# A gated feed-forward kernel: a load of x that waits for a memset, and fillers of another size

## The chip, the cores and the metric

The kernel runs on one core of a Trainium2 chip. The core has five engines with a queue each: TensorE (PE; its weight loads are listed apart as PEld), VectorE (DVE), ScalarE (ACT), GpSimd (POOL) and SyncE (SP). Transfers between the chip's memory and the core's on-chip memory are issued by an engine's queue (here SP and ACT) and carried out by 16 DMA engines. The metric is the device time of one execution in microseconds (us): 163.03 us before, the median of 3 runs that went from 162.87 to 163.18.

## The reference

```python
def reference(x, w_gate, w_up, w_down):
    g = _silu(x @ w_gate)
    u = x @ w_up
    return (g * u) @ w_down
```

All arrays are bf16: x is 1 x 2048 x 640 (S = 2048 rows, D = 640), w_gate and w_up are 640 x 1536 (F = 1536), w_down is 1536 x 640.

## The kernel before

**Tiles.** The 2048 rows are worked in four blocks of 512 (`sb`). D is cut into five parts of 128 (`kd`), F into twelve of 128 (`fc`, `kf`). For each block and each fc, line 197 (`proj`) adds up five matmuls of 512 columns for the gate (`pg`) and five for the up projection (`pu`); line 214 takes the silu on ScalarE, line 215 multiplies on VectorE into `aT`. After twelve fc the block is multiplied with `w_down` (lines 273 and 302), copied and stored. Beside this VectorE works out the last four rows of x by dot products (line 150).

TensorE needs x turned, with D on the partitions (`xT`). Rows 0 to 255 are loaded as they lie, into `x_sb` (line 85: rows 0 to 127 from SyncE's queue, rows 128 to 255 from ScalarE's), and turned by TensorE against an identity (line 188, five transposes for each 128 rows); ScalarE and VectorE copy the result to `xT` (line 193). The rest of x is turned by the transfer itself (line 109, `turn_x`).

**The order at the start**, which the change touches:

- SyncE's queue: x rows 0 to 127 (line 85); w_gate kd = 0 and, after it, kd = 1 and kd = 4, each for the first four fc (line 120); the turned x rows 256 to 511 (line 109); then w_up (line 82), the rest of w_gate and w_up, and w_down (line 128).
- ScalarE's queue: x rows 128 to 255 (line 85); w_gate kd = 2 and 3 in one transfer (line 120); then a silu on one column of `ones` (line 122), which makes ScalarE load its table early; then its share of the copies (line 193).
- VectorE: the memset of `ones` (line 105), then its copies (line 193).
- TensorE, an order written out by hand in `head` and fixed by `keep_order`: the fillers (`warm`, line 179), matmuls of `ones` with itself whose result nobody reads; ten transposes; the kd = 0 matmuls of the first four fc, first for rows 0 to 127 and then for rows 128 to 255 (line 240, 128 columns); kd = 1 to 4 for rows 0 to 255 (line 240, 256 columns); the same four fc for rows 256 to 511 (line 197, 256 columns); then w_up for these fc (line 197).

The fillers wait for the memset, the transposes for x, line 240 for w_gate and the copies. The function `_trim` takes away the barrier at the beginning, so each engine starts its queue by itself.

Of the kernel before, what the change touches and what calls it, by code (L numbers as in the profile page):

```python
# [10 lines left out]
def _body(  # L11
# [8 lines left out]
    nc = tc.nc  # L20
    P = nc.NUM_PARTITIONS
    f32 = mybir.dt.float32
    bf16 = mybir.dt.bfloat16
    ACT = mybir.ActivationFunctionType
# [10 lines left out]
    S_BLK = 512  # L35
# [1 line left out]
    SUB = S_BLK // P  # L37
    DA = 512
    Q = 32
    N_WARM, N_EARLY = 18, 4  # L40
    T = 4
    WT_STEP = 4
    PE_X = 2
# [4 lines left out]
    consts = ctx.enter_context(tc.tile_pool(name="consts", bufs=1))  # L48
# [7 lines left out]
    x_sb = consts.tile([P, PE_X, D], bf16)  # L56
# [15 lines left out]
    x_v = x2.rearrange("(c p) d -> p c d", p=P)  # L72
# [5 lines left out]
    def wslice(a, b):  # L78
        return slice(a * P, b * P)

    def load_w(eng, dst, src, a, b):
        eng.dma_start(out=dst[:, :, wslice(a, b)], in_=src[:, :, wslice(a, b)])

    def load_x(eng, c0, c1):
        eng.dma_start(out=x_sb[:, c0:c1, :], in_=x_v[:, c0:c1, :])  # L85

    def issue_order(a, b):
        tc.add_manual_dep(
# [8 lines left out]
    def keep_order(engine):  # L97

        traced = [i for i in nc.cur_bb.bb.instructions if i.engine == engine]
        for a, b in zip(traced, traced[1:]):  # L100
            issue_order(a, b)

    ones = consts.tile([P, P], bf16)
    silu_first = consts.tile([P, 1], f32)
    nc.vector.memset(ones[:], 1.0)  # L105

    def turn_x(c0, c1):
        s_sl = slice(c0 * P, c1 * P)
        nc.sync.dma_start_transpose(out=xT[:, :, s_sl], in_=xt_v[s_sl])

    f_sl = wslice(0, N_EARLY)
    load_x(nc.sync, 0, 1)
    load_x(nc.scalar, 1, 2)
    for eng, k0, k1 in (
        (nc.sync, 0, 1),
        (nc.scalar, 2, 4),
# [2 lines left out]
    ):  # L119
        eng.dma_start(out=wg_sb[:, k0:k1, f_sl], in_=wg_v[:, k0:k1, f_sl])  # L120
    turn_x(PE_X, SUB)
    nc.scalar.activation(silu_first[:], ones[:, 0:1], ACT.Silu)
    load_w(nc.sync, wu_sb, wu_v, 0, N_EARLY // 2)
    load_w(nc.sync, wu_sb, wu_v, N_EARLY // 2, N_EARLY)
    for a, b in W_CHUNKS:
# [6 lines left out]
    def turn_w(dst, src):  # L132
# [7 lines left out]
        out=x_row[:],  # L140
        in_=x2[S - T : S, :].rearrange("t d -> (t d)").partition_broadcast(P),
# [32 lines left out]

    pw = psum.tile([P, S_BLK], f32, tag="gu", name="pw", bufs=4)

    def warm(n):
        for _ in range(n):
            nc.tensor.matmul(  # L179
                pw[:, 0:P], lhsT=ones[:], rhs=ones[:], start=True, stop=True  # L180
            )

    def transpose_chunk(c, parts):
        c_sl = slice(c * P, (c + 1) * P)
        for copy, tag, k0, k1 in parts:
            pt = psum.tile([P, k1 - k0, P], bf16, tag=tag, name="pt")
            for kd in range(k0, k1):
                nc.tensor.transpose(  # L188
                    out=pt[:, kd - k0, :],
                    in_=x_sb[:, c, kd * P : (kd + 1) * P],  # L190
                    identity=ident[:],
                )
            copy(out=xT[:, k0:k1, c_sl], in_=pt[:])  # L193

    def proj(ps, w_sb, fc, sb, c0, c1):
        for kd in range(KD):
            nc.tensor.matmul(  # L197
                ps[:, c0:c1],
                lhsT=w_sb[:, kd, fc * P : (fc + 1) * P],
                rhs=xT[:, kd, sb * S_BLK + c0 : sb * S_BLK + c1],  # L200
                start=(kd == 0),
                stop=(kd == KD - 1),
            )
# [6 lines left out]
    def gate(pg, pu, sb, fc, n_s):  # L210

        s0 = sb * S_BLK
        sg = work.tile([P, S_BLK], f32, name="sg")
        nc.scalar.activation(sg[:, 0:n_s], pg[:, 0:n_s], ACT.Silu)  # L214
        nc.vector.tensor_tensor(  # L215
            out=aT[:, fc, s0 : s0 + n_s], in0=sg[:, 0:n_s], in1=pu[:, 0:n_s], op=ALU.mult
        )

    def head():

        dve, act = nc.vector.tensor_copy, nc.scalar.copy
        split = [(act, "po_a", 0, 2), (dve, "po_b", 2, KD)]
        late = PE_X * P
        warm(N_WARM)
        transpose_chunk(0, split)
        transpose_chunk(1, split)  # L230
        pg = [
            psum.tile([P, S_BLK], f32, tag="gu", name="pg", bufs=4)
            for _ in range(N_EARLY)
        ]
        early = [(0, 0, P), (0, P, late)] + [(kd, 0, late) for kd in range(1, KD)]
        for kd, c0, c1 in early:
            for fc in range(N_EARLY):


                nc.tensor.matmul(  # L240
                    pg[fc][:, c0:c1],
                    lhsT=wg_sb[:, kd, wslice(fc, fc + 1)],
                    rhs=xT[:, kd, c0:c1],
                    start=(kd == 0 and c0 == 0),
                    stop=(kd == KD - 1),
                )
        for fc in range(N_EARLY):
            proj(pg[fc], wg_sb, fc, 0, late, S_BLK)
        for fc in range(N_EARLY):
            pu = psum.tile([P, S_BLK], f32, tag="po_b" if fc % 2 else "po_a", name="pu")  # L250
            proj(pu, wu_sb, fc, 0, 0, S_BLK)
            gate(pg[fc], pu, 0, fc, S_BLK)
        keep_order(mybir.EngineType.PE)
        keep_order(mybir.EngineType.Activation)

    head()
    for sb in range(NSB):
        n_s = S_BLK if sb < NSB - 1 else S_BLK - T
# [13 lines left out]
        for kf in range(KF):  # L272
            nc.tensor.matmul(  # L273
                po_t[:],
                lhsT=wd_sb[:, kf, DA:D],
                rhs=aT[:, kf, sb * S_BLK : sb * S_BLK + n_t],
                start=(kf == 0),
                stop=(kf == KF - 1),
# [6 lines left out]
        for q in range(P // Q):  # L285
            nc.scalar.dma_start(
                out=out2[
                    sb * S_BLK : sb * S_BLK + n_t, DA + q * Q : DA + (q + 1) * Q
                ].rearrange("(i r) c -> r i c", r=Q),
                in_=ot_q[q * Q : (q + 1) * Q, :].rearrange("r (i c) -> r i c", c=Q),  # L290
            )

        for j in range(SUB):
            s0 = sb * S_BLK + j * P
            last = sb == NSB - 1 and j == SUB - 1
            cols = [(0, DA, "po_a")]
            if last:
                cols = [(0, DA // 2, "po_a"), (DA // 2, DA, "po_a"), (DA, D, "po_b")]
            for c0, c1, tag in cols:
                po = psum.tile([P, c1 - c0], f32, tag=tag, name="po_a")  # L300
                for kf in range(KF):
                    nc.tensor.matmul(  # L302
                        po[:],
                        lhsT=aT[:, kf, s0 : s0 + P],
                        rhs=wd_sb[:, kf, c0:c1],
                        start=(kf == 0),
                        stop=(kf == KF - 1),
                    )
                ot = outp.tile([P, c1 - c0], bf16, name="ot" if c1 < D else "ot_b")
                if c1 < D:  # L310
                    nc.scalar.copy(ot[:], po[:])  # L311
                    eng = nc.sync
                else:
                    nc.vector.tensor_copy(out=ot[:], in_=po[:])  # L314
                    eng = nc.scalar
# [81 lines left out]
def kernel(tc, *args):  # L397
    _body(tc, *args)
    tc.close()
    tc.compile()  # L400
    _trim(tc.nc)
# [30 lines left out]
```

## Time and profile before

| what | us |
|---|---|
| median of 3 runs | 163.03 |
| profiled execution, device time | 163.16 |
| profiled execution, span from first to last instruction | 161.8 |
| TensorE busy (share of the span) | 158.9 (98%) |
| VectorE busy | 110.9 (69%) |
| ScalarE busy | 42.7 (26%) |
| 18 fillers on TensorE (line 179), from 0.40 | 2.10 |
| memset of `ones` on VectorE (line 105) | 0.165 |

The span begins with SyncE's first issue, at 0.00. The profile is one execution, taken by the hardware profiler. Times in its views are us from the start of the span; "idle before, releaser" says how long an engine stood still and what ended that. Matmuls are pipelined, so the length of one is more than the distance from one start to the next. The chain of waits is followed back from the last instruction: at each step to what released it, or to the instruction before it on its engine.

### The profile page before, as it was taken

How to read it: one execution, taken by the hardware profiler on the slowest of the kernel's cores; microseconds unless marked ns; L12 is line 12 of the kernel's file. 1: busy time of each engine (PE TensorE's matmuls, PEld its weight loads, DVE VectorE, ACT ScalarE, POOL GpSimd, SP SyncE). 2: the span in 40 equal slices, each digit the busy share in tenths (PEclk: the TensorE clock that was granted, in tenths of full speed). 3: DMA queues.
4: the chain of work that ended last, by engine and by line, in shares of the span. 5: the costliest groups of instructions: out<-in, count | busy, mean ns of one | idle time of the engine just before them, and what ended most of it. 6: DMA issues, size and time to landing. Idle time of an engine off the chain costs nothing.

```text
span 161.8 us, 2113 instructions
## 1 busy us (share of the span) xinstructions
PE 158.9 (98%) x796; PEld 77.1 (48%) x796; DVE 110.9 (69%) x249; ACT 42.7 (26%) x74; POOL 0.6 (0%) x6
## 2 busy tenths in 40 slices
PE   8999999999999999999999999999999999999995
PEld 7754444444444444444444444444444444445454
DVE  1035223599469999989919999979964999993000
ACT  5131222112222222211222322221214222222121
POOL 1000000000000000000000000000000000000000
DMA  7999999995189991003110000000321000000312
GB/s 226 265 344 350 363 218 231 245 189 101 35 186 166 228 226 39 4 0 34 65 65 0 0 4 2 0 0 4 61 67 34 0 0 0 0 0 4 50 39 73
DMA packets 41801, 15.86 MB, mean 98 GB/s; under 512 B 33216, under 2 KB 41664, under 8 KB 41792
## 3 DMA queue, kind: packets, MB, share of 16 engines
q1 hardware_dynamic: 33296, 14.78, 38.0%
q10 hardware_dynamic: 8496, 0.95, 3.9%
q8 instruction: 6, 0.10, 0.3%
q14 instruction: 3, 0.02, 0.1%
HBM read 6.88 MB, written 2.62 MB: 59 GB/s over the span
## 4 chain that ended last, share of the span: by engine, by line
PE 96%; DMA 2%; SPq 1%; DVE 0%; issue 0%
PE pu L197 32%; PE pg L197 31%; PE po_a L302 26%; PE po_t L273 6%; DMA wg_sb<-in_w_gate_dram 2%; PE pg L240 1%; SPq L120 0%; SPq L85 0%; DVE ot_b L314 0%
## 5 line engine op out<-in xcount | busy, mean ns | idle before, releaser
L197 PE MATMUL pu<-xT,wu_sb 128*128 128x512 bf16 (+1 forms) x240 | 59.0, 379 | 0.0
L197 PE MATMUL pg<-xT,wg_sb 128*128 128x512 bf16 (+2 forms) x240 | 56.9, 370 | 0.0
L215 DVE TENSOR_TENSOR aT<-sg,pu 128x512 bf16<-128x512 f32 (+1 forms) x48 | 32.8, 683 | 32.3 <-PE pu L197 32.3
L214 ACT ACTIVATE sg<-pg 128x512 f32<-128x512 f32 (+1 forms) x48 | 28.5, 596 | 70.7 <-PE pg L197 65.7
L302 PE MATMUL po_a<-wd_sb,aT 128*128 128x512 bf16 (+2 forms) x216 | 42.8, 358 | 0.0
L150 DVE SCALAR_TENSOR_TENSOR prod<-wgT,x_row 128x640 f32<-128x640 bf16 x48 | 39.4, 821 | 1.1
L150 DVE SCALAR_TENSOR_TENSOR prod<-wuT,x_row 128x640 f32<-128x640 bf16 x48 | 39.5, 822 | 1.0
L197 PEld LDWEIGHTS <-wu_sb 128*128 128x128 bf16 x240 | 23.5, 98 | 28.0
L197 PEld LDWEIGHTS <-wg_sb 128*128 128x128 bf16 x240 | 23.5, 98 | 26.1
L302 PEld LDWEIGHTS <-aT 128*128 128x128 bf16 x216 | 20.7, 98 | 21.7
L311 ACT CAST ot<-po_a 128x512 bf16<-128x512 f32 (+1 forms) x17 | 9.5, 560 | 32.0 <-PE po_a L302 20.9
L273 PE MATMUL po_t<-aT,wd_sb 128*128 128x512 bf16 (+1 forms) x48 | 10.4, 366 | 0.0
L273 PEld LDWEIGHTS <-wd_sb 128*128 128x128 bf16 x48 | 4.7, 98 | 5.1
L314 DVE CAST ot_b<-po_a 128x128 bf16<-128x128 f32 x1 | 0.3, 292 | 9.9 <-PE po_a L302 9.9
L282 ACT CAST ot_t<-po_t 128x512 bf16<-128x512 f32 (+1 forms) x4 | 2.2, 558 | 11.6 <-PE po_t L273 11.6
L150 DVE DVE_READ_ACCUMULATOR prod<-wuT,x_row 128x1 f32 x48 | 4.0, 83 | 0.0
L150 DVE DVE_READ_ACCUMULATOR prod<-wgT,x_row 128x1 f32 x48 | 4.0, 82 | 0.0
L284 DVE STREAM_TRANSPOSE ot_q<-ot_t 128x512 bf16<-128x512 bf16 (+1 forms) x4 | 2.7, 678 | 1.7 <-ACT ot_t L282 1.7
L240 PE MATMUL pg<-xT,wg_sb 128*128 128x256 bf16 (+1 forms) x24 | 2.6, 255 | 0.4 <-DMA wg_sb<-in_w_gate_dram 0.4
L193 DVE COPY xT<-pt 128x384 bf16<-128x384 bf16 x2 | 0.7, 358 | 3.2 <-PE pt L188 3.1
L179 PE MATMUL pw<-ones 128*128 128x128 bf16 x18 | 2.1, 313 | 0.4 <-DVE ones L105 0.4
L240 PEld LDWEIGHTS <-wg_sb 128*128 128x128 bf16 x24 | 1.9, 98 | 0.8 <-DMA wg_sb<-in_w_gate_dram 0.7
(15 smaller groups left out, 7.7 us busy)
## 6 DMA issues: line engine op xcount, KB each, us to landing
wd_sb<-in_w_down_dram SPq DMA_DIRECT2D x1, 1920.0 KB, 13.6
out_dram<-ot SPq DMA_DIRECT2D x15, 128.0 KB, 1.7
wg_sb<-in_w_gate_dram SPq DMA_DIRECT2D x2, 640.0 KB, 8.0
wu_sb<-in_w_up_dram SPq DMA_DIRECT2D x2, 640.0 KB, 8.6
wu_sb<-in_w_up_dram SPq DMA_DIRECT2D x2, 320.0 KB, 5.1
x_row<-in_x_dram SPq DMA_DIRECT2D x1, 640.0 KB, 5.0
wg_sb<-in_w_gate_dram SPq DMA_DIRECT2D x3, 128.0 KB, 3.8
out_dram<-ot_q ACTq DMA_DIRECT2D x12, 32.0 KB, 1.9
```

The lines of the kernel that those rows point to most:

```text
L150: nc.vector.scalar_tensor_tensor(out=prod[:], in0=wT[:, fc, :], scalar=1.0, in1=x_row[:, t, :], op0=ALU.mult, op1=ALU.mult, accum_out=acc[ ...
L179: nc.tensor.matmul(pw[:, 0:P], lhsT=ones[:], rhs=ones[:], start=True, stop=True)
L193: copy(out=xT[:, k0:k1, c_sl], in_=pt[:])
L197: nc.tensor.matmul(ps[:, c0:c1], lhsT=w_sb[:, kd, fc * P : (fc + 1) * P], rhs=xT[:, kd, sb * S_BLK + c0 : sb * S_BLK + c1], start=(kd == 0 ...
L214: nc.scalar.activation(sg[:, 0:n_s], pg[:, 0:n_s], ACT.Silu)
L215: nc.vector.tensor_tensor(out=aT[:, fc, s0 : s0 + n_s], in0=sg[:, 0:n_s], in1=pu[:, 0:n_s], op=ALU.mult)
L240: nc.tensor.matmul(pg[fc][:, c0:c1], lhsT=wg_sb[:, kd, wslice(fc, fc + 1)], rhs=xT[:, kd, c0:c1], start=(kd == 0 and c0 == 0), stop=(kd == ...
L273: nc.tensor.matmul(po_t[:], lhsT=wd_sb[:, kf, DA:D], rhs=aT[:, kf, sb * S_BLK : sb * S_BLK + n_t], start=(kf == 0), stop=(kf == KF - 1),)
L282: nc.scalar.copy(ot_t[:], po_t[:])
L284: nc.vector.transpose(out=ot_q[:], in_=ot_t[:])
L302: nc.tensor.matmul(po[:], lhsT=aT[:, kf, s0 : s0 + P], rhs=wd_sb[:, kf, c0:c1], start=(kf == 0), stop=(kf == KF - 1),)
L311: nc.scalar.copy(ot[:], po[:])
```

## The change

ScalarE's load of x rows 128 to 255 gets a dependency on VectorE's memset, so ScalarE's queue stands until the memset is done. The memset now fills one column (`one`, 128 x 1) where it filled 128 (`ones`, 128 x 128). The fillers read that column with a step of zero, as a 128 x 128 weight and as 512 or 128 columns of the moving operand; there are four of 512 columns and two of 128 where there were eighteen of 128. The early silu reads the one column.

```diff
-    N_WARM, N_EARLY = 18, 4
+    N_LONG, N_WARM, N_EARLY = 4, 2, 4
...
-    ones = consts.tile([P, P], bf16)
+    one = consts.tile([P, 1], bf16)
     silu_first = consts.tile([P, 1], f32)
-    nc.vector.memset(ones[:], 1.0)
+    one_set = nc.vector.memset(one[:], 1.0)
...
     load_x(nc.sync, 0, 1)
-    load_x(nc.scalar, 1, 2)
+    x1 = load_x(nc.scalar, 1, 2)
+
+    tc.add_manual_dep(
+        x1.ins,
+        one_set.ins.name,
+        mybir.DependencyInfo(mybir.DependencyClass.Sync, mybir.DependencyReason.DATA),
+        reason="x0_first",
+    )
...
-    nc.scalar.activation(silu_first[:], ones[:, 0:1], ACT.Silu)
+    nc.scalar.activation(silu_first[:], one[:], ACT.Silu)
...
-    def warm(n):
+    def warm(n, cols):
         for _ in range(n):
             nc.tensor.matmul(
-                pw[:, 0:P], lhsT=ones[:], rhs=ones[:], start=True, stop=True
+                pw[:, 0:cols],
+                lhsT=one[:].to_broadcast([P, P]),
+                rhs=one[:].to_broadcast([P, cols]),
+                start=True,
+                stop=True,
             )
...
-        warm(N_WARM)
+        warm(N_LONG, S_BLK)
+        warm(N_WARM, P)
```

`load_x` returns the instruction, which it did not before.

More of the change, by code (lines that the diff above doesn't have):

```diff
@@ L84, in load_x @@
     def load_x(eng, c0, c1):
-        eng.dma_start(out=x_sb[:, c0:c1, :], in_=x_v[:, c0:c1, :])
+        return eng.dma_start(out=x_sb[:, c0:c1, :], in_=x_v[:, c0:c1, :])
     def issue_order(a, b):
```

## The prediction

> **What bounds the kernel now.** I read the chain of waits first, because the change touches only the first 3 us and what matters is whether they lie on the path that sets the end.
>
> ```profile
> 0.00 0.40 SPq L85
> ...
> 0.46 0.41 SPq L120
> ...
> 0.91 3.89 DMA wg_sb<-in_w_gate_dram
> 4.80 0.05 issue
> 4.85 1.92 PE pg L240 x16
> 6.77 2.18 PE pg L197 x20
> 8.95 4.32 PE pu L197 x20
> ```
>
> The columns are start, length, owner. Until 4.80 us the path is SyncE's queue and one transfer: the second 128 rows of w_gate (kd = 1), issued at 0.91, landed at 4.80. From 4.85 on TensorE is the chain, without a hole, to 159.91. So only two things can move the end: a new landing time of that transfer, or a new pace or hole in TensorE's stream behind it. The timeline of the first microseconds shows what the change touches:
>
> ```profile
> 0.12 0.40 ACTq L85 DMA_DIRECT2D x_sb<-in_x_dram  x1
> 0.17 0.17 DVE L105 MEMSET ones<- 128x128 bf16 x1 [0.17 <-issue]
> ...
> 0.40 2.10 PE L179 MATMUL pw<-ones 128*128 128x128 bf16 x18 [0.40 <-DVE ones L105]
> ...
> 0.55 0.45 ACTq L120 DMA_DIRECT2D wg_sb<-in_w_gate_dram  x1
> ...
> 1.03 1.28 ACT L122 ACT_TABLE_LOAD   x1 [1.03 <-issue]
> ...
> 2.71 1.16 PE L188 MATMUL pt<-ident,x_sb 128*128 128x128 bf16 x10 [0.21 <-DMA x_sb<-in_x_dram]
> ...
> 3.84 0.64 PE L240 MATMUL pg<-xT,wg_sb 128*128 128x128 bf16 x8
> ```
>
> Fillers, transposes and the eight kd = 0 matmuls end at 4.32 (the last starts at 4.26 and follows at 0.055), so TensorE stands idle for 0.48 us before kd = 1 lands. That idle stretch is the cover of everything the change delays. The DMA issues give the landings (last column: us from issue to landing):
>
> ```profile
> wg_sb<-in_w_gate_dram SPq DMA_DIRECT2D x3, 128.0 KB, 3.8
> ...
> wg_sb<-in_w_gate_dram ACTq DMA_DIRECT2D x1, 256.0 KB, 4.1
> x_sb<-in_x_dram SPq DMA_DIRECT2D x1, 160.0 KB, 2.7
> x_sb<-in_x_dram ACTq DMA_DIRECT2D x1, 160.0 KB, 2.9
> ```
>
> By the trace's semaphore records: x rows 0 to 127 land at 2.66, rows 128 to 255 at 3.04, w_gate kd = 0 at 3.80, kd = 2 and 3 (ScalarE's) at 4.69, kd = 1 at 4.80, the turned x (line 109) at 6.41.
>
> **The wait, part by part.** The memset shrinks from 128 columns to one. No one-column memset of VectorE is in the trace. From above it is the 0.165 us of line 105; from below the 128x1 accumulator read, 0.08 us; GpSimd's 128x1 memsets take 0.10. I take 0.08, a row of the same engine and width. It ends at 0.17 + 0.08 = 0.25 (at the latest 0.34). TensorE started 0.06 after the memset ended; I give ScalarE the same. Its x load is then issued at 0.31 instead of 0.12: **0.19 us later**, at most 0.28. Queued behind it on ScalarE, all 0.19 later:
> - The x load itself: landing 3.04 + 0.19 = 3.23. Its transposes come after the five of the first chunk, at 3.21. They wait 0.02, at most 0.11; the kd = 0 matmuls then end at 4.34 to 4.43, still before 4.80. Cost 0; without the 0.48 of cover, 0.02 to 0.11.
> - The w_gate load kd = 2 and 3: landing 4.88, at most 4.97. It is first read four kd = 1 matmuls (0.109 apart) after 4.85, at 5.28. Cost 0 with 0.3 to spare.
> - The table load and first silu: end at 2.72 instead of 2.53. ScalarE's first copy starts at 3.14. Cost 0.
>
> SyncE's issues are not moved. But kd = 1 shares the 16 DMA engines with 416 KB of ScalarE's, and they are full from 1 us on:
>
> ```profile
> 1.00:2.00 1.00, 1.00 (x13) 1.00 (x11) 0.00 (x0) 0.97 (x1) 0.00 (x0) 1.00 0.87 227
> 2.00:3.00 1.00, 0.79 (x8) 0.53 (x7) 0.00 (x0) 0.52 (x2) 0.00 (x0) 1.00 1.02 331
> ```
>
> The last two columns are the share of the 16 engines and GB/s. Bounds: if SyncE's transfers use the whole stretch that ScalarE's leave, kd = 1 lands up to 0.28 earlier; if the engines run dry for as long, up to 0.28 later. I take 0: by the packet records the first ScalarE packet starts at 1.52, just as the first of x's 16 parts is done, and the packets of each transfer follow those of the one issued before. New issue starts are 0.00 (x), 0.31 (x, ScalarE), 0.46 (kd = 0), 0.74 (kd = 2, 3, ScalarE), 0.91 (kd = 1): the same order. x's first packet came 1.03 after its issue began, so the delayed load can start at 1.34, before the 1.52 at which an engine is free. The wait would be hidden in that queue.
>
> The Trainium skill (DMA: Bandwidth & Descriptors, "Queues, rings and completion order") says otherwise: each engine alternates between the queues by packets. By that rule SyncE's transfers gain while ScalarE's is held back, and kd = 1 comes up to that delay earlier; the packet records, with ScalarE's first at 1.52, do not show the alternation.
>
> An earlier kd = 1 is soon met by the next wait: line 197's first matmuls start at 6.61 and read the turned x, landed at 6.41. A lead over 0.19 us turns into a wait there unless that transfer moves as well.
>
> **The fillers.** 4 x 512 + 2 x 128 = 2304 columns, as 18 x 128 = 2304 before. Spacing before: (2.10 - 0.31) / 17 = 0.105 per 128 columns (0.31 is the length of one). No 512-column matmul at that pace is in the trace. By columns it is 0.42; from below the later 512-column spacing, 0.216; from above the 0.38 length of one with no overlap, times 0.105 / 0.055 for the early pace, 0.73. A single column read again and again is in no row; these ends stand for it. I take 0.42, since both known sizes go by columns: 4 x 0.42 + 2 x 0.105 = 1.89, so last start plus length end at 0.31 + 1.89 + 0.21 = 2.41 instead of 2.50. The x chunk lands at 2.66: hidden, **cost 0**. Twelve pairs of weight load and matmul less: 0, they lie before 2.5.
>
> **Sum**: 0 on the profiled execution: 163.16 us (span 161.8 and 1.36 around it). The median of the runs is 163.03, 0.13 below, so I say **163.0**.
>
> **Rivals.**
> 1. *Faster: the first transfer, alone for longer, leaves no straggler.* kd = 1 lands in 16 parts: 14 by 4.48, the last two at 4.73 and 4.80. Parts of x show the same (15 by 2.34, the last at 2.66). If the 0.32 lag starts in the crowd at 1 to 2 us and goes, and the turned x, queued on the same engines, comes earlier too, the gain is 0.32 to 0.48 (the idle before 4.80). For: x's straggler. Against: packets of x already take over 0.4 us at 1.1 us, before ScalarE's appear. About -0.38: 162.65.
> 2. *Slower: the matmul pace opens late.* The spacing changes from 0.105 to 0.055 between transposes and line 240, about 3.84 - 0.40 = 3.44 after the first filler. The gap ahead of the transposes grows from 0.21 to 0.29. It decides if that gap restarts the count: change at 2.71 + 3.44 = 6.15, so 4.85 to 6.15 goes slowly and loses 1.3 x (1 - 0.055/0.105) = 0.62: 163.65. Against: the runs lie within 0.31 of each other.
> 3. *Slower: the fillers overrun.* At 0.73 each: 0.31 + 2.92 + 0.62 = 3.85, transposes 1.15 late; the last four kd = 0 matmuls (now 4.09 to 4.32) end at 5.47, 0.62 past 4.85, or near 0 if the transposes then run at the fast pace. About +0.45: 163.5.
> 4. *The wait does nothing,* because the memset is done when ScalarE comes to its load: same time as the forecast, part of it.
>
> The skill's clock page (TensorE: Matmul & The Clock Gate, Part 1) speaks for rival 2: the clock doubles only after about 3.4 us of busy window, and the window runs free of the kernel. Run-to-run variation as it describes would be wider than the 0.31 of these runs; if it held, the opening moment would not depend on the change, and the forecast stays.
>
> **How the numbers follow.** A measurement of this kernel tells 0.2% (0.33 us) from no change. Forecast with rival 4: 0.58, within 162.75 to 163.31 by the bound of 0.28 on the transfer. Rival 1: 0.24, faster by over 0.2%. Rival 2: 0.10 and rival 3: 0.08, slower. The range takes in the forecast's bounds, rival 1 down to its -0.48 (162.5) and rival 3 to 163.5; rival 2 and the far end of 3 are left out, under 0.2.
>
> **What would show it.** In the changed profile: ScalarE's x load issued at about 0.3; the chain still through w_gate's kd = 1 with TensorE's line 240 (256 columns) from 4.8 to 4.9; fillers over about 1.9 us ending before the transposes; line 240's 128-column matmuls still short (0.22). Wrong if line 240 starts its 256-column part by 4.5 (rival 1), if its matmuls take over 0.3 there (rival 2), or if the transposes wait for TensorE and not for x (rival 3).

## The result, and the profile after

The changed kernel takes **163.85 us** (median of 7 runs, 163.43 to 164.38), the kernel before 163.03 in the same runs (162.82 to 163.29). The ratio is 1.0038, with a 95% interval of 1.0019 to 1.0056: slower by 0.4% (the two medians alone lie 0.5% apart). The profiled execution took 163.65, 0.49 more than that of before, with a span of 162.2. In all ratios here, executions more than 1.5% above the fastest of their kernel are left out; the traces of wait_18, wait_long and split are of such executions, and only their transfers are read.

The chain of waits of the changed kernel, over its first 10 us (start, length, owner):

```profile
0.91 4.10 DMA wg_sb<-in_w_gate_dram
5.01 0.05 issue
5.05 2.02 PE pg L252 x16
7.08 2.27 PE pg L208 x20
```

It is the chain of before with later times: w_gate kd = 1 lands at 5.01 instead of 4.80, and the stretch up to the first w_up matmul takes 0.19 longer. The timeline shows what the change did to the start:

```profile
0.14 0.06 DVE L105 MEMSET one<- 128x1 bf16 x1
0.23 0.39 ACTq L85 DMA_DIRECT2D x_sb<-in_x_dram  x1
0.30 2.10 PE L186 MATMUL pw<-one 128*128 128x512 bf16 x6 [0.30 <-DVE one L105]
...
0.66 0.45 ACTq L127 DMA_DIRECT2D wg_sb<-in_w_gate_dram  x1
...
2.35 1.25 PE L199 MATMUL pt<-ident,x_sb 128*128 128x128 bf16 x10
```

ScalarE's x load is held by 0.11 only (0.12 to 0.23), its w_gate load kd = 2 and 3 with it (0.55 to 0.66). The fillers are as long as before. The transposes start 0.36 earlier. The DMA issues (last column: us from issue to landing):

```profile
wg_sb<-in_w_gate_dram SPq DMA_DIRECT2D x3, 128.0 KB, 4.1
...
wg_sb<-in_w_gate_dram ACTq DMA_DIRECT2D x1, 256.0 KB, 4.9
x_sb<-in_x_dram SPq DMA_DIRECT2D x1, 160.0 KB, 2.3
x_sb<-in_x_dram ACTq DMA_DIRECT2D x1, 160.0 KB, 2.5
```

Both x loads are faster than before (2.3 for 2.7, 2.5 for 2.9), and so is w_gate kd = 0 behind them; the other w_gate loads are slower (the 4.1 is the median of SyncE's three), ScalarE's most (4.9 for 4.1). By the semaphore records, before and after:

| transfer | lands before | lands after |
|---|---|---|
| x rows 0 to 127 | 2.66 | 2.30 |
| x rows 128 to 255 | 3.04 | 2.74 |
| w_gate kd = 0 | 3.80 | 3.06 |
| kd = 1 | 4.80 | 5.01 |
| kd = 2 and 3 | 4.69 | 5.55 |
| kd = 4 | 5.15 | 5.75 |
| turned x, rows 256 to 511 | 6.41 | 6.96 |

A transfer has landed when the last of its 16 parts has. By the same records it is a few parts that come late: of kd = 1, 14 had landed by 4.48 before and the last two at 4.73 and 4.80; after, 11 by 4.46 and five from 4.83 to 5.01. Of kd = 2 and 3, 11 had landed by 4.77 after, and five from 5.48 to 5.55.

With it goes a drop of the transfer rate. In the table by stretches, 2.5 to 3.5 us, first of the kernel before and then of the changed one (last two columns: share of the 16 DMA engines, GB/s):

```profile
2.50:3.50 1.00, 0.79 (x8) 0.80 (x9) 0.04 (x1) 0.39 (x2) 0.00 (x0) 1.00 0.95 309
```

```profile
2.50:3.50 1.00, 1.00 (x12) 1.00 (x11) 0.36 (x1) 0.70 (x3) 0.00 (x0) 1.00 0.71 199
```

From 309 to 199 GB/s, with the engines' share down from 0.95 to 0.71. The changed kernel was ahead at 2.5 (0.44 MB moved, against 0.40) and behind at 4.5 (0.92 against 1.05). The packet records show in what order: w_gate goes in packets of 1 KB, 128 for kd = 0, 128 for kd = 1 and 256 for kd = 2 and 3. Before, the 129th of SyncE's, which can't be of kd = 0, starts at 3.31, and ScalarE's kd = 2 and 3 starts 164 of its packets between 2.50 and 3.25. After, SyncE's 129th starts at 2.65, in the midst of kd = 2 and 3, which starts only 81 in that time. SyncE starts about as many in it as before (52 and 51), so the two queues together start 133 packets instead of 215.

In the matmul starts this costs 0.21 by kd = 1, 0.10 in a second wait at 5.39 (for kd = 2 and 3, landed at 5.55) and 0.09 in a third at 6.81 (for the turned x, landed at 6.96): together 0.40. The first w_up matmul starts at 9.19 instead of 8.79, which is that 0.40. The other 0.09 of the 0.49 lie after it or outside the span.

**From this start to the end all kernels are alike.** The device time of each profiled execution, less the start of its first w_up matmul:

| kernel | first w_up matmul | device us | difference |
|---|---|---|---|
| before | 8.79 | 163.16 | 154.37 |
| after | 9.19 | 163.65 | 154.46 |
| no_wait | 9.20 | 163.66 | 154.46 |
| w23_mid | 8.61 | 163.07 | 154.46 |
| wait_alone | 9.68 | 164.07 | 154.39 |
| w23_late2 | 10.71 | 165.17 | 154.46 |
| turn_later | 10.94 | 165.39 | 154.45 |

So all that is to be explained happens before the first w_up matmul, and one trace for each kernel is enough to see what happened in that execution, not how often it does.

### The profile page after: what moved, and what is told of

It reads as the page before. It is cut to its first block, busy times and chain, and to the rows that moved or that the text cites. A ratio compares the mean times of both kernels' runs of the same rounds, so it can differ in the third digit from the quotient of the medians.

```text
span 162.2 us, 2089 instructions
## 1 busy us (share of the span) xinstructions
PE 159.2 (98%) x784; PEld 76.3 (47%) x784; DVE 110.7 (68%) x249; ACT 42.7 (26%) x74; POOL 0.6 (0%) x6
## 4 chain that ended last, share of the span: by engine, by line
PE 96%; DMA 3%; SPq 0%; DVE 0%; issue 0%
PE pu L208 32%; PE pg L208 31%; PE po_a L314 26%; PE po_t L285 6%; DMA wg_sb<-in_w_gate_dram 3%; PE pg L252 1%; SPq L127 0%; SPq L85 0%; DVE ot_b L326 0%
## 5 line engine op out<-in xcount | busy, mean ns | idle before, releaser
L186 PE MATMUL pw<-one 128*128 128x512 bf16 (+1 forms) x6 | 2.1, 523 | 0.3 <-DVE one L105 0.3
```

The source lines that it names most:

```text
L186: nc.tensor.matmul(pw[:, 0:cols], lhsT=one[:].to_broadcast([P, P]), rhs=one[:].to_broadcast([P, cols]), start=True, stop=True,)
```

## The experiments

"w23" in the labels is ScalarE's load of w_gate kd = 2 and 3. Each kernel was profiled once and timed against the kernel before on the same chip, most with 12 executions. The kernel before had medians from 163.20 to 163.33 in these sets, with single executions from 162.71 to 165.66.

### Which part of the change is it?

Four kernels take the change apart. `no_wait` is the changed kernel without its `add_manual_dep`. The others:

```diff
 # wait_alone, on the kernel before
-    nc.vector.memset(ones[:], 1.0)                     # 128 columns
+    one_set = nc.vector.memset(ones[:], 1.0)
...
-    load_x(nc.scalar, 1, 2)
+    x1 = load_x(nc.scalar, 1, 2)
+    tc.add_manual_dep(x1.ins, one_set.ins.name, ...)
 # wait_18, on the changed kernel; no_wait_18 is wait_18 without the dependency
-    N_LONG, N_WARM, N_EARLY = 4, 2, 4
+    N_WARM, N_EARLY = 18, 4
...
-        warm(N_LONG, S_BLK)
         warm(N_WARM, P)
```

no_wait: 

> The changed kernel without the dependency: one column of ones, four fillers of 512 and two of 128 columns, ScalarE's x load free to start. Theory Q (the wait pushes ScalarE's queue back, so its w_gate transfer kd 2 and 3 runs side by side with SyncE's kd 1 and both land late): time as before, 163.0, kd 1 landed at about 4.8. Theory F (the fillers are the cause, by a later change of the matmul pace or by what they do to the transfers): as after, 163.8.

wait_alone: 

> The kernel before, with the dependency alone: 128-column memset, eighteen fillers. ScalarE's x load issued at about 0.40. Theory Q: as after or somewhat more, 163.8 to 164.0, kd 2 and 3 landed past 5.2. Theory F: as before, 163.0.

wait_18: 

> The changed kernel with eighteen fillers of 128 columns on the one column; the dependency stays. Theory Q: as after, 163.8. Theory F, if the 512 columns are the cause: as before, 163.0; if the column read with a step of zero is the cause: 163.8.

no_wait_18: 

> One column of ones and eighteen fillers of 128 columns on it, no dependency: only the small memset and the step of zero are left of the change. Theory Q: as before, 163.0. Theory F: 163.0 if the 512 columns are the cause, 163.8 if the step of zero is.

Measured: no_wait 163.40, ratio 1.0005 (0.9989 to 1.0020); no_wait_18 163.40, 1.0004 (0.9986 to 1.0022); wait_18 163.83, 1.0038 (1.0015 to 1.0062); wait_alone 164.06, 1.0027 (0.9992 to 1.0062), wide, with four of twelve executions above 165, so that it shows nothing by itself. **The wait is the cause**: after and no_wait, and wait_18 and no_wait_18, differ in nothing else, and in both pairs the kernel without the wait is back at the time of the kernel before. The small memset, the column read with a step of zero and the 512-column fillers cost nothing that can be measured. The rate from 2.5 to 3.5 goes with it: 329 and 360 GB/s without the wait, 260 and 237 with it.

### Which of the two held loads?

The wait holds everything on ScalarE's queue. `w23_late` frees the x load and holds only kd = 2 and 3, by a second memset of VectorE; w23_late2 and w23_mid differ from it in the memset's columns.

```diff
 # on no_wait
+    pause = consts.tile([P, 360], bf16)     # w23_late2: 840, w23_mid: 640
+    paused = nc.vector.memset(pause[:], 0.0)
...
-        eng.dma_start(out=wg_sb[:, k0:k1, f_sl], in_=wg_v[:, k0:k1, f_sl])
+        w = eng.dma_start(out=wg_sb[:, k0:k1, f_sl], in_=wg_v[:, k0:k1, f_sl])
+        if k0 == 2:
+            tc.add_manual_dep(w.ins, paused.ins.name, ...)
```

w23_late: 

> The changed kernel with the wait moved: ScalarE's x load is free, and its w_gate load (kd 2 and 3) waits for a second memset of VectorE, 360 columns, so that it is issued at about 0.66 as in the changed kernel. Theory W (what costs is that this load comes closer to SyncE's kd 1 and the two then share the engines packet by packet at a lower rate): 163.6 to 163.9, kd 2 and 3 landed after 5.1, 180 to 260 GB/s between 2.5 and 3.5. Theory X (what costs is the late x load, which leaves the engines short of work after the first chunk): 163.3, as without the wait, over 300 GB/s there.

Its memset took 0.21, was done at 0.43 and held nothing: the load went out at 0.56 as in no_wait. It only repeats no_wait: 163.74, ratio 1.0018 (0.9982 to 1.0054), 364 GB/s. That its median lies 0.4 above that of the kernel before, with nothing held, shows how far such a set can stray.

w23_late2: 

> As w23_late, with a second memset of 840 columns, since the one of 360 took 0.21 and held nothing back: ScalarE's x load is free (issued at 0.12), only kd 2 and 3 is issued at about 0.66, as in the changed kernel. Theory W (this load's lead over SyncE's kd 1 is what counts): 180 to 290 GB/s between 2.5 and 3.5, kd 2 and 3 landed after 5.1, time 163.7 to 164.0. Theory X (the late x load is what counts): over 310 GB/s there, 163.3.

Measured: 163.87, ratio 1.0035 (1.0014 to 1.0055). ScalarE's queue and the stretch from 2.5 to 3.5 in its trace:

```profile
0.12 0.38 ACTq L85 DMA_DIRECT2D x_sb<-in_x_dram  x1
...
0.70 0.39 ACTq L123 DMA_DIRECT2D wg_sb<-in_w_gate_dram  x1
```

```profile
2.50:3.50 1.00, 1.00 (x10) 1.00 (x11) 0.26 (x1) 0.54 (x3) 0.00 (x0) 1.00 0.97 263
```

x goes out at 0.12 as before, kd = 2 and 3 at 0.70, and the median is 0.56 above the kernel before. A late x load (theory X) is not needed for that; the late w_gate load is enough. It is slower than the kernel before, but not clear of w23_late, whose interval overlaps. And the trace does not show how the time is lost: kd = 2 and 3 landed at 4.78 (expected: after 5.1), kd = 1 at 4.97 and the turned x at 6.45, all within 0.17 of before; it had moved 0.42 MB by 2.5, against 0.40 before, and 0.69 against 0.71 by 3.5. This execution took 165.17, one of two above 165, by the pace of its matmuls (below).

w23_mid: 

> As w23_late2 with a memset of 640 columns: ScalarE's x load free, kd 2 and 3 issued at about 0.60 to 0.62. If the loss grows in step with the issue time: 163.5 to 163.6, 280 to 320 GB/s from 2.5 to 3.5. If it sets in past a point later than this: 163.3, over 320 GB/s; if past an earlier one: 163.8, under 290.

Measured: 163.54, ratio 1.0007 (0.9993 to 1.0020).

```profile
0.61 0.39 ACTq L123 DMA_DIRECT2D wg_sb<-in_w_gate_dram  x1
```

```profile
2.50:3.50 1.00, 0.98 (x10) 0.98 (x11) 0.22 (x1) 0.41 (x3) 0.00 (x0) 1.00 1.01 339
```

At 0.61 there is no loss that can be measured and no drop of the rate. The means of the executions below 165 are 163.41 in no_wait, 163.47 in w23_mid, 163.61 in w23_late and 163.80 in w23_late2. All kernels that leave SyncE's loads of the head as they are and ScalarE's in their order and size:

| kernel | kd 2, 3 issued | GB/s, 2.5 to 3.5 | kd 2, 3 lands | kd 1 lands |
|---|---|---|---|---|
| before_fill | 0.54 | 364 | 4.08 | 5.06 |
| no_wait_18 | 0.55 | 360 | 4.00 | 5.00 |
| before | 0.55 | 309 | 4.69 | 4.80 |
| no_wait | 0.56 | 329 | 4.64 | 4.42 |
| w23_late | 0.56 | 364 | 4.21 | 4.55 |
| w23_mid | 0.61 | 339 | 4.72 | 4.45 |
| after | 0.66 | 199 | 5.55 | 5.01 |
| no_silu | 0.66 | 180 | 5.93 | 5.40 |
| wait_18 | 0.67 | 260 | 5.20 | 5.16 |
| after_fill | 0.68 | 235 | 5.70 | 5.22 |
| w23_late2 | 0.70 | 263 | 4.78 | 4.97 |
| wait_alone | 0.83 | 237 | 5.59 | 5.02 |
| wait_long | 0.96 | 265 | 6.42 | 5.43 |

No trace with kd = 2 and 3 issued by 0.61 is below 309, none from 0.66 on is above 265, and the rate does not fall in step between them (the kernels not met yet follow below). The packet records part the same two groups: SyncE's 129th packet starts at 3.15 to 3.31 in the first six and at 2.57 to 2.86 in the other seven. That the time has a step too is not shown, with the intervals of w23_mid and w23_late2 overlapping. Nor does the landing of kd = 1 tell the groups apart by itself: it is 5.00 and 5.06 in two kernels without a wait, where 15 parts had landed by 4.35 and 4.57.

wait_long holds x by a memset of 470 columns (issued at 0.52), on the changed kernel. 

> The changed kernel with a longer wait: ScalarE's x load waits for a second memset of 470 columns, is issued at about 0.75, and kd 2 and 3 at about 1.18, after the issue of kd 1 has begun. Theory W: SyncE's kd 1 is now ahead, lands by 4.5, kd 2 and 3 land at 5.3 or later; time 163.5 to 164.0. Theory X: the stretch without work grows to 0.5 and the loss with it, 164.2 or more, with kd 1 past 5.2.

Measured: 164.45, ratio 1.0048 (1.0007 to 1.0088), with five of twelve executions above 164.8. kd = 1, though issued ahead of kd = 2 and 3 (0.91 and 0.96), landed at 5.43, 15 of its parts by 4.43 and the last 1.00 later. Theory W missed with kd = 1 and with the time, theory X met both: a long hold of x may cost by itself, which no run separates.

### What beside the late load lowers the rate?

kd1_later gives kd = 2 and 3 its lead over SyncE's kd = 1 back, by holding kd = 1 as well; kd1_far holds it to 1.88. Both use the memset and dependency shown above, on the changed kernel:

```diff
+    pause = consts.tile([P, 1700], bf16)     # kd1_far: 3080
...
+        if k0 == 1:
+            tc.add_manual_dep(w.ins, paused.ins.name, ...)
```

kd1_later: 

> The changed kernel, wait and all, in which SyncE's kd 1 also waits, for a memset of 1700 columns, and is issued at about 1.02 instead of 0.91. Theory W: kd 2 and 3 has its lead of 0.35 back, the rate between 2.5 and 3.5 is over 300 GB/s again and both land by 4.9: 163.1 to 163.4, a wait more and yet faster than the changed kernel. Theory X, or that any delay adds: 163.8 to 164.0.

Measured: 163.80, ratio 1.0049 (1.0013 to 1.0086); kd = 1 issued at 1.16; 292 GB/s; kd = 2 and 3 landed at 5.89, kd = 1 at 5.35. The lead does not bring the landings back: that part of theory W falls. SyncE's 129th packet, at 2.93, still started among those of kd = 2 and 3.

kd1_far: 

> The changed kernel with SyncE's kd 1 held until about 1.7, so that kd 2 and 3 (issued at 0.67) has the engines to itself after kd 0. If packets of kd 1 beside it lower the rate: kd 2 and 3 lands by 4.5, the rate is over 300 GB/s from 2.5 to 3.3; kd 1 lands at about 5.2 and the turned x late, so the time is still 163.8 to 164.3. If the late issue by itself does: kd 2 and 3 lands past 5 again, and the time is 164.2 or more.

Measured: 163.94, ratio 1.0053 (1.0033 to 1.0072); kd = 2 and 3 landed at 5.12.

```profile
2.50:3.50 1.00, 1.00 (x11) 1.00 (x10) 0.36 (x1) 0.70 (x3) 0.00 (x0) 1.00 0.79 247
```

kd = 1 was not issued before 1.88, and the rate is as low. By the rate and the landing that speaks for the late issue alone, but the packet records do not: SyncE started no packet of 1 KB between 2.75 and 3.25, so the stretch is short of work, and kd = 2 and 3 started 154 of its packets from 2.50 to 3.25, nearly the 164 of the kernel before and not the 81 of the changed one. Its late landing is that of the last parts (12 by 4.03, the last at 5.12), after kd = 1 had come in at 3.26. So packets of kd = 1 among those of kd = 2 and 3 remain a likely part of the cause.

turn_later holds the turned x in the same way, by a memset of 5300 columns. 

> The changed kernel with SyncE's turned x load (rows 256 to 511) and all behind it held until about 2.6 instead of 1.86. If its issue, which runs while kd 2 and 3 begin, lowers the rate: over 300 GB/s from 2.5 to 3.5, both w_gate loads by 4.9; the turned x lands at about 7, 0.5 late: 163.5 to 163.9. If not: the rate stays at 180 to 290 and the time is 164.0 to 164.6.

Measured: 164.04, ratio 1.0058 (1.0038 to 1.0078).

```profile
2.50:3.50 1.00, 1.00 (x11) 0.98 (x12) 0.82 (x2) 0.63 (x3) 0.00 (x0) 1.00 0.91 258
```

The turned x, now issued at 3.04, is not the cause: in the changed kernel too its first packet started at 4.09 only.

```diff
 # split, on the changed kernel
-        (nc.scalar, 2, 4),
+        (nc.scalar, 2, 3),
+        (nc.scalar, 3, 4),
```

split: 

> The changed kernel with ScalarE's load of kd 2 and 3 cut into two loads of 128 KB. If one large load late in the queue is what runs slowly: kd 2 lands before 4.9, 163.3 to 163.6. If the late issue counts: kd 3, issued at about 1.1, is later still: 163.8 to 164.2.

Measured: 163.65, ratio 1.0013 (0.9997 to 1.0030), with eight executions from 162.94 to 163.71 and four from 165.40 to 165.57: inconclusive. 277 GB/s; kd = 2 landed at 4.32, kd = 3 at 5.81.

no_silu takes the line `nc.scalar.activation(silu_first[:], one[:], ACT.Silu)` out of the changed kernel; the result of that silu is read by nobody. 

> The changed kernel without the early silu on the one column (its result is read by nobody), so that ScalarE's table load comes with its first copy, at about 2.3 to 2.7, and the copies a table load later. Only the rate is asked: if the table load beside the transfers lowers it, over 310 GB/s from 2.5 to 3.0 and kd 2 and 3 landed before 5.0. If not, under 290 there. Time 164 or more either way, since the copies come 1 us later.

Measured: 163.94, ratio 1.0054 (1.0025 to 1.0083), 180 GB/s. The edit missed its aim: a table load still came at 1.14, and a second one at 3.63. Whether the table load matters was not tested.

### Would another order be better?

```diff
 # w23_first, on no_wait: ScalarE issues kd 2 and 3, then x
 # kd1_act, on no_wait
-        (nc.scalar, 2, 4),
-        (nc.sync, 1, 2),
+        (nc.scalar, 1, 2),
+        (nc.sync, 2, 4),
 # one_x, on the kernel before
-    load_x(nc.sync, 0, 1)
-    load_x(nc.scalar, 1, 2)
+    load_x(nc.sync, 0, 2)
```

w23_first: 

> No wait, six fillers on the one column, and ScalarE issues kd 2 and 3 first (0.12) and x rows 128 to 255 second (0.57). Theory W: kd 2 and 3 is well apart from kd 1, kd 1 lands by 4.8, time 163.0 to 163.4, the second chunk's transposes wait for x and are hidden. Theory X: the x load is even later than in the changed kernel, 163.8 or more.

Measured: 165.43, ratio 1.0124 (1.0065 to 1.0184). The rate is the best of all, 383 GB/s, kd = 2 and 3 landed at 3.18. But x rows 128 to 255, issued at 0.60, landed at 4.05, and TensorE stood 0.95 before their transposes: a late x is not hidden once it is 1 us late.

kd1_act: 

> No wait, six fillers on the one column; ScalarE loads kd 1 after its x, and SyncE loads kd 2 and 3 in place of kd 1. If the order of issue is the order of landing when nothing is held back, kd 1 (issued at 0.55) lands at about 4.2 and kd 2 and 3 at 4.7 to 4.9; the four kd 1 matmuls fill 0.44 of the hole, and the turned x at 6.4 leaves 0.2 of that: 162.9 to 163.2. If the queues' packets alternate whatever the order, as after: 163.6.

Measured: 163.79, ratio 1.0007 (0.9977 to 1.0037). kd = 1 landed at 3.66, but kd = 2 and 3 at 5.46; the stand moved behind the kd = 1 matmuls.

one_x: 

> The kernel before with both x chunks in SyncE's first load (320 KB), so that ScalarE's first issue is kd 2 and 3, at 0.12. If the rate rises with an earlier issue of it: over 340 GB/s from 2 to 3.5, kd 1 landed by 4.6, x by 3.0: 162.7 to 163.2, at or below the kernel before. If not: x's first chunk lands with the second, all of the head is later by 0.3, 163.4 to 163.8.

Measured: 164.57, ratio 1.0075 (1.0048 to 1.0101). The rate was high (359) and kd = 1 landed at 4.54, but x only at 3.30. No version beat the kernel before.

### The pace of the matmuls

```diff
 # after_fill on the changed kernel, before_fill on the kernel before (with ones)
         for kd, c0, c1 in early:
+            if kd == 1:
+                pf = psum.tile([P, S_BLK], f32, tag="po_a", name="pf")
+                for _ in range(6):
+                    nc.tensor.matmul(pf[:, 0:P], ...)   # a filler
```

after_fill: 

> The changed kernel with six more fillers of 128 columns between the kd 0 and the kd 1 matmuls. Theory G (beside the late transfers, the stand of 0.8 to 1.0 before kd 1 makes the fast matmul pace come a whole stretch of about 3.4 later in some executions): median 163.5 to 163.8, nothing above 164.6. If only the late transfers count: as the changed kernel, 163.8, with the same spread or 0.2 more, as the fillers overrun kd 1 in executions with the slow pace.

before_fill: 

> The kernel before with six more fillers of 128 columns between the kd 0 and the kd 1 matmuls, where it stands 0.4 to 0.5. Theory G: the same median, 163.1 to 163.4, with fewer executions above 163.7. If the stand plays no part: the same or up to 0.2 more.

Measured: after_fill 164.08 (163.79 to 164.32, 8 runs), ratio 1.0036 (1.0022 to 1.0051); before_fill 163.61 (162.85 to 164.16), 1.0010 (0.9994 to 1.0027). Fillers in the hole gain nothing in either. No execution of these two lies above 164.4, as theory G had it, but none of the seven of the changed kernel does either, and both medians lie above what it said (163.8 and 163.4 at most): the theory is not shown.

That the pace matters, and differs between executions, is plain in the traces. Line 240's sixteen matmuls of 256 columns, in no_wait (all 24 in one row, eight of them of 128 columns), and in w23_late2:

```profile
3.58 3.60 PE L246 MATMUL pg<-xT,wg_sb 128*128 128x128 bf16 x24
```

```profile
5.01 3.59 PE L257 MATMUL pg<-xT,wg_sb 128*128 128x256 bf16 x16 [0.42 <-DMA wg_sb<-in_w_gate_dram]
```

The same sixteen took 2.02 in the changed kernel, with a wait of 0.10 in them, and 1.92 before. By the starts of the matmuls, the spacing of 256 columns is 0.213 early and 0.109 later. The change came at 3.7 in the kernel before, at 3.9 in the changed one, 6.0 in no_wait, 3.6 in no_wait_18, 4.4 in w23_mid, 6.4 in wait_alone, 8.5 in w23_late2, 8.9 in turn_later. In no_wait kd = 1 landed 0.38 earlier than before and the first w_up matmul came 0.41 later, by this pace alone. In w23_late2 the slow pace from 5.01 to 8.5 costs 3.5 x (1 - 0.109 / 0.213) = 1.7, which is why that execution took 165.17. The other traced executions between 165.0 and 165.4 (one_x, no_silu, turn_later) changed between 8.2 and 9.1. Executions above 165 are none of 24 in no_wait and no_wait_18, two of twelve in wait_18 and four in wait_alone, but also two in w23_mid and none of seven in the changed kernel; whether a wait makes a late change more frequent was not tested.

## Why the prediction was wrong

The forecast was no change, 163.0, with a range to 163.5; the median is 163.85 and the sign is slower.

1. **What bounds the kernel: right.** The chain still runs through SyncE's kd = 1 into TensorE's stream, and the time of every traced execution is the start of its first w_up matmul plus 154.4 to 154.5.
2. **The length of the wait: mis-sized, without harm.** The memset took 0.06 (taken: 0.08) and ScalarE followed 0.03 after it (taken: 0.06): 0.11 instead of 0.19.
3. **The fillers: right.** 2.10 us at 0.43 per 512 columns (taken: 0.42), done at 2.40 (2.41). Rival 3 fell with it, and so did every part of the change but the wait.
4. **The step that failed: "The same order... The wait would be hidden in that queue", cost 0.** It let the packets of each transfer follow those of the one issued before, and so treated each transfer as shifted by at most the delay of its issue. The issues kept their order, the packets did not: SyncE's go past kd = 0 at 2.65 instead of 3.31, and kd = 2 and 3 starts 81 packets where it started 164. The alternation of queues that the prediction set aside is nearer to this. The kernel before already spoke against a strict order: between 1.5 and 2.0, 59 packets of SyncE's x load start beside 54 of ScalarE's. For kd = 1 the bounds of 0.28 either way held (+0.21). For kd = 2 and 3 I wrote 4.88, at most 4.97; it landed at 5.55. The turned x I used only as a limit to gains; it came 0.55 late and became a wait. In the traced executions a delay of 0.11 went with 110 GB/s less for a microsecond, and over all traces the rate goes with the issue time of kd = 2 and 3, changing between 0.61 and 0.66. That the wait costs the time is shown; how the late issue lowers the rate stays open.
5. **Rival 1 was half right.** The straggler of x went (2.66 to 2.30), as it said, and kd = 0 came 0.74 earlier. But kd = 1 had more late parts than before, five for two, and nothing on the path waits for x or kd = 0; TensorE's stand before kd = 1 only grew from 0.5 to 0.9.
6. **Rival 2: the price was real, the reason was not.** The late change of pace costs what it was reckoned at, and more (1.7 in w23_late2), but it is not set off by the gap before the transposes: no_wait and no_wait_18 have fillers and a gap of the same length and changed at 6.0 and 3.6. The Trainium skill (TensorE: Matmul & The Clock Gate, Part 1) says that the window which opens the clock runs free of the kernel, so that the same kernel opens at different moments. I set that aside because the first runs lay within 0.31. The traces fit that, with each kernel traced once: the moment varies by microseconds among kernels whose fillers take the same 2.10 us, and single executions of the kernel before range from 162.71 to 165.66. The page gives the variation as 0.5 us either way; here the moments lie up to 5 us apart, and the measurement decides. Three runs were too few to argue from.

**What stays open.** Why the rate drops. The turned x (turn_later) is not needed for it; the packets of SyncE's kd = 1 among those of the late load are not ruled out by kd1_far, and why the two together should run slower than one after the other is not shown. The Trainium skill (DMA: Bandwidth & Descriptors, "Issuing engines are not separate DMA queues") says that issuing from several engines saves only issue time, which is usually small beside the transfer. It is here (0.45 of issue, 4.1 to the landing), and yet a shift of 0.11 on one queue cost 0.4%: small beside the transfer was not small for the time. ScalarE's table load, which follows the issue by 0.03 in the head of before and after, was not separated from it. How much of the median's 0.8 is transfers and how much is pace can't be told from one trace for each kernel: the 0.40 is shown for the profiled execution alone. Nor was the changed kernel timed again in the later sets, where the kernel before had medians 0.2 to 0.3 higher than the 163.03 it is compared with.

## What to carry to other kernels

A wait on a queue is paid by everything queued behind it, and a transfer does not shift by the delay of its issue: ask what the rate of the whole stream will be, and watch the landing that is read last, part by part, not the one that the wait was meant to help. Before calling an edit of the first microseconds free, find out how far the time varies by itself, from many executions, and look in each trace for where the dense stretch begins; here that one number gave the end to within 0.1 us.

## What the runs showed of the hardware that was not expected

- Issued at 0.61 or earlier, ScalarE's 256 KB load ran in a stream of 309 to 364 GB/s; issued at 0.66 to 0.96, the stream of the same transfers ran at 180 to 265 GB/s from 2.5 to 3.5, with SyncE's next packets (kd = 1) in at 2.57 to 2.86 instead of 3.15 to 3.31.
- The spacing of matmuls halves at a moment that differs by 5 us between executions (3.6 to 8.9), while the granted clock that the profile lists is 1.00 in every stretch, so that the column does not show it; the starts of the matmuls do.
- A memset of 360 columns of bf16 took 0.21, and is listed as 180 columns of 32 bits: half the elements, and a wait built on it held nothing.
- SyncE's x load arrived without its straggler when ScalarE's was held: 16 parts by 2.30 instead of 15 by 2.34 and the last at 2.66. In the ten traces with ScalarE's x load held it landed at 2.23 to 2.42, in the eight with that load issued at 0.12 or 0.13 at 2.44 to 2.67.
